# Batch 2's q and k loaded plain, cast by GpSimd and transposed on TensorE in a fused attention and MLP kernel

## The chip, the cores and the metric

The kernel runs on one core of one Trainium2 chip. The metric is the time of an execution on the device in microseconds (us); lower is better. The core's engines are TensorE (PE, with its weight loads counted apart as PEld), VectorE (DVE), ScalarE (ACT), GpSimd (POOL) and SyncE (SP, which here only issues DMAs). Each engine takes its instructions in the order in which the program wrote them, and waits where an operand isn't there yet.

## The reference

There are 8 batches of 8 heads, a sequence of 576 and a head dimension of 64, all inputs in float32. Per head:

```python
scores = q @ k.T / sqrt(64)
cum    = cumsum(log(clip(f, 1e-4, 1)))
scores = where(causal, -1e9, scores + cum[:, None] - cum[None, :])
attn   = softmax(scores)
out    = attn @ v
```

The heads of a token are put side by side, which gives x with 4608 rows of 512. Then `h = x @ w_in` (512 to 2048), `g = h * sigmoid(h)` and `g @ w_out` (2048 to 512), written in float32.

## The kernel before

**Units of work.** Attention goes by pairs of heads: pair p is batch p // 4, heads 2 (p % 4) and the next, 32 pairs in all. The MLP goes by groups of 512 tokens, 9 groups. A group has 16 parts of the first product (`m1_chunk`: four matmuls into hp at L397, tanh on ACT, one DVE instruction at L409 that writes gtile) and 16 parts of the second (`m2_part`: four matmuls into po at L422; every fourth part ends in a copy on ACT and an output store from SP, L435).

**Attention of a pair.** `scores` makes four score tiles (0 to 3): matmuls of kT by qT (L278), the exponential on ACT (L303), the causal mask on DVE (L317). `prep_v` on POOL multiplies v by the decay weights (L248). `attend_rows` is the product with v (L346), the division on DVE, and `turn_pair` transposes the result on PE (L368) and has ACT copy it into xT (L374). Group g of the MLP can start when xT of all its tokens is written: group 0 after batch 0, group 1 after batch 1, and so on.

**How q and k get into qT and kT.** Both need the head dimension on the partitions and bf16. There are two ways.

- Batches 0 and 1: `load_main` loads tokens 0 to 511 of q and k in float32 from SP's queue (L98) into `whole`, a buffer of the pool gpool under the tag gtile, which has two buffers and is shared with the MLP's gtile. `load_tail` does the same for the last 64 tokens (L107, two buffers). `cast_both(p)` has POOL cast a pair's share to bf16 (L190 for whole, L199 for the tails). `transposes(p, which)` makes five PE transposes (L232) and two DVE copies (L237, L241) of one of q and k.
- Batches 2 to 7: `load_qk` loads blocks of 128 tokens from POOL's queue with a cast to bf16 in the DMA (L123, into mp, 16 buffers); `turn_qk` issues a DMA transpose of a block from SP (L132) into qT or kT. A batch has five blocks, the last of 64 tokens, so ten casting loads and ten DMA transposes.

**The order around the change.** From pair 4 on, the loop over p writes out for each pair: what `plan` holds for p (DMA transposes and loads of v, all on SP); score tiles 0 and 1; n1 parts of the MLP; for pairs of batches 0 and 1, `transposes(p + 1, 0)`; `attend_rows(p - 1)` for the lower rows; `prep_v(p + 1)`; `cast_both(p + 2)` while p + 2 is below 8; what `fetch` holds for p (the casting loads, on POOL); score tiles 2 and 3; `transposes(p + 1, 1)`; and the rest of the MLP parts and of attention of the pair before. From batch 2 on, `attend_rows(p - 1)` comes after score tile 3 in one piece. `pace` sets how many MLP parts a pair gets, from the parts that are ready. For batch 2 the loads stand in fetch at pairs 4 (blocks 0, 1) and 5 (blocks 2 to 4), the transposes in plan at 6 (blocks 0, 1) and 7; for batch 3 the loads at 5, 6, 7 and the transposes at 8, 9, 10. The loads of v for batch 2 stand in plan at 4 (blocks 0, 1), 5 (block 2) and 6 (blocks 3, 4).

PSUM has four buffers under the tag big (pool pbig) for hp, po, the attention products and the transposes, and two for the score tiles.

Of the kernel before, what the change touches and what calls it, by code (L numbers as in the profile page):

```python
# [19 lines left out]
def kernel(  # L20
# [12 lines left out]
    B, H, S, D = q.shape  # L33
# [9 lines left out]
    NPB = H // 2  # L43
# [28 lines left out]
    tpool = ctx.enter_context(tc.tile_pool(name="tpool", bufs=3))  # L72
    opool = ctx.enter_context(tc.tile_pool(name="opool", bufs=4))
    NEARLY = 2
    NTURN = 4
    LAG = 10.0
    MOST = 9.0
# [8 lines left out]
    def raw_tile():  # L86
        return stp.tile([P, DM], FP32, name="raw", tag="raw")
# [4 lines left out]
    def load_main(b, h0, h1):  # L92
        if b not in whole:
            whole[b] = gpool.tile(
                [P, 2, H, (NB - 1) * D], FP32, name="whole", tag="gtile"
            )
        for which, src in enumerate((q, k)):
            nc.sync.dma_start(  # L98
                out=whole[b][:, which, h0:h1, :],
                in_=src[b, h0:h1, 0:SM, :].rearrange("h (p c) d -> p h (c d)", c=NB - 1),  # L100
            )

    def load_tail(b):
        for which, src in enumerate((q, k)):
            t = raw_tile()
            tails[b, which] = t.rearrange("s (h d) -> s h d", h=H)
            nc.sync.dma_start(  # L107
                out=tails[b, which][:TAIL, :, :],
                in_=src[b, :, SM:S, :].rearrange("h s d -> s h d"),
            )  # L110
# [86 lines left out]
    def cast_tail(b, j, which):  # L197
        m = cast[b, j, which]
        nc.gpsimd.tensor_copy(  # L199
            out=m[:TAIL, NB - 1, :, :], in_=tails[b, which][:TAIL, 2 * j : 2 * j + 2, :]  # L200
        )
# [236 lines left out]
    m2_queue = [(g, tb, pt) for g in range(NG) for tb in range(4) for pt in range(4)]  # L438
    m1_ready = 0
# [16 lines left out]
    def can_m1():  # L456
        if not m1_queue:
            return False
        g = m1_queue[0][0]
        return g < m1_ready and (not m2_queue or m2_queue[0][0] > g - 2)  # L460

    def can_m2():
        return bool(m2_queue) and (not m1_queue or m1_queue[0][0] > m2_queue[0][0])
# [14 lines left out]
    def have():  # L478
        return sum(1 for x in m1_queue + m2_queue if x[0] < m1_ready)

    def pace(p):
        b, j = divmod(p, NPB)
        if b < NEARLY:
            return have() / (NPB - j)
# [32 lines left out]
    def add(to, at, fn, *args):  # L517
        to.setdefault(at, []).append(lambda: fn(*args))

    for b in range(NEARLY, B):  # L520
        for i, group in enumerate([(0, 1), (2,), (3, 4)]):
            at = NPB * b - 4 + min(i, 1) if b == NEARLY else NPB * b - 7 + i
            for c in group:
                for w in range(2):
                    add(fetch, at, load_qk, b, c, w)
                    if b <= NEARLY + 1:
                        add(plan, at + (2 if b == NEARLY else 3), turn_qk, b, c, w)
                    elif i == 0 and b - 2 >= NTURN:
                        add(plan, NPB * b - 4, defer, 9.0, partial(turn_qk, b, c, w))
                    else:  # L530
                        add(plan, NPB * b - 4 + min(i, 1), turn_qk, b, c, w)
                add(plan, NPB * b - 5 + i + (b == NEARLY), load_v, b, c, nc.sync)

# [11 lines left out]
    with tc.manual_schedule():  # L545
        nc.scalar.dma_start(out=f_sb[:, :], in_=f.rearrange("b h s -> (b h) s"))
        load_main(0, 0, 2)
        load_tail(0)
        load_main(0, 2, 4)
        for c in range(2):  # L550
            load_v(0, c, nc.sync)
        load_main(0, 4, H)
        for c in range(2, NB):
            load_v(0, c, nc.sync)

        def cast_both(p):
            b, j = divmod(p, NPB)
            for w in range(2):
                cast_main(b, j, w)
            for w in range(2):  # L560
                cast_tail(b, j, w)

        make_identity(nc, ident_bf)
        make_upper_triangular(nc, mask01, val=1.0, diag=True)
        make_identity(nc, ident_f)
        for kT in kTs:
            nc.vector.memset(kT[:, :, S:], 0.0)
        for u in us:
            nc.vector.memset(u[:, :, uoff[4] + TAIL :], 0.0)
        for va in vaugs:  # L570
            nc.vector.memset(va[:, NB - 1, :, :], 0.0)
        nc.vector.memset(wT[:, NB - 1, :], 0.0)
        nc.vector.tensor_scalar(
            out=maskadd[:, :], in0=mask01[:, :], scalar1=1.0, scalar2=1e30,
            op0=ALU.subtract, op1=ALU.mult,
        )
        decay_clip()
        LO, HI = ((0, 3),), ((3, NB),)
        for w in range(2):
            cast_main(0, 0, w)  # L580
        for w in range(2):
            cast_tail(0, 0, w)
        cast_both(1)
        cast_both(2)
        load_w(w_in_bf, moe_w_in, 0, DFF // 2)
        load_w(w_in_bf, moe_w_in, DFF // 2, DFF)
        for w in range(2):
            turn_first(w)
        scores(0, 0)
        turn_first_tails()  # L590
        scores(0, 1)
        decay_sum()
        scores(0, 3)
        transposes(1, 0)
        scores(0, 2)
        decay_turn()
        prep_v(0)
        transposes(1, 1)
        scores(1, 0)
        cast_both(3)  # L600
        load_tail(1)
        load_main(1, 0, 4)
        load_main(1, 4, H)
        for c in range(NB):
            load_v(1, c, nc.sync)
        for p in range(1, NPB):
            more = p + 1 < NPB
            prep_v(p)
            scores(p, 1)
            if more:  # L610
                transposes(p + 1, 0)
            scores(p, 3)
            if more:
                transposes(p + 1, 1)
            if p > 1:
                turn_pair(p - 2)
            attend_rows(p - 1, LO)
            scores(p, 2)
            if more:
                scores(p + 1, 0)  # L620
            attend_rows(p - 1, HI)
        turn_pair(NPB - 2)
        attend_rows(NPB - 1, LO)
        attend_rows(NPB - 1, HI)
        m1_chunk(0, 0, begin=True)
        turn_pair(NPB - 1)
        m1_ready = 1
        cast_both(NPB)
        cast_both(NPB + 1)
        prep_v(NPB)  # L630
        for c in range(0, NFC, NFC // 4):
            load_rows(w_out_bf, moe_w_out, c, c + NFC // 4)
        work(HOLD)
        transposes(NPB, 0)
        work(1)
        transposes(NPB, 1)
        work(2)
        due = 0.0
        for p in range(NPB, NP):
            b, j = divmod(p, NPB)  # L640
            early = b < NEARLY
            for fn in plan.get(p, []):
                fn()
            due += pace(p)
            n = int(due)
            due -= n
            n1, n2 = (n + 2) // 3, (n + 1) // 3
            n3 = n - n1 - n2
            scores(p, 0)
            scores(p, 1)  # L650
            spend(0.4)
            work(n1)
            ahead = p + 1 < NPB * NEARLY
            rows = NPB < p < NPB * NEARLY
            if ahead:
                transposes(p + 1, 0)
            if rows:
                attend_rows(p - 1, LO)
                spend(0.6)
            if p + 1 < NP:  # L660
                prep_v(p + 1)
            if p + 2 < NPB * NEARLY:
                cast_both(p + 2)
            for fn in fetch.get(p, []):
                fn()
            if early:
                work(n2 // 2)
            scores(p, 2)
            scores(p, 3)
            spend(0.3)  # L670
            if ahead:
                transposes(p + 1, 1)
            if rows:
                attend_rows(p - 1, HI)
            work(n2 - n2 // 2 if early else n2)
            if b >= NEARLY and j > 0:
                attend_rows(p - 1)
                spend(1.2)
            work(n3)
            if j > 0 and b < NTURN:  # L680
                turn_pair(p - 1)
            if j == NPB - 1:
                attend_rows(p)
                spend(1.2)
                if b < NTURN:
                    work(2)
                    turn_pair(p)
                    ready(p)
                else:
                    retire(p)  # L690
        while m1_queue or m2_queue or later:
            n = len(m1_queue) + len(m2_queue)
            work(1)
            if n == len(m1_queue) + len(m2_queue):
                spend(1.0)
# [28 lines left out]
```

## Time and profile before

| what | value |
|---|---|
| median of 3 runs | 363.94 us (363.58 to 365.53) |
| the profiled execution: time | 366.61 us |
| the profiled execution: span from the first to the last instruction | 364.8 us |
| granted TensorE clock, mean | 0.984 |
| busy: PE, PEld | 339.6 us (93%), 167.1 us (46%) |
| busy: DVE, ACT, POOL | 189.7 us (52%), 212.1 us (58%), 120.5 us (33%) |
| chain that ended last | PE 75%, DMA 10%, SP's queue 7% |

All times below are from the start of the span. The view of 40 slices gives the busy share of each engine in tenths for each fortieth of the span (9.12 us), and the clock that the throttle granted to TensorE. A line of the timeline has the start, the duration from the first to the last instruction of a merged group, the engine, the line of the kernel, the operation, what it writes and reads (partitions x elements and type), how often, and in brackets the idle time before it with what ended it. A line of the waits has the waiting instruction, what it waited for, the sum in us, how many times, and the longest. Matmuls overlap, so the pace of a group is read from start to start. Pairs can be found in PE's timeline by their first score tile (64x512): pair 4 at 41.78, 5 at 49.46, 6 at 59.06, 7 at 67.72, 8 at 82.70, 9 at 95.10, 10 at 103.50, 12 at 123.22.

### The profile page before, as it was taken

How to read it: one execution, taken by the hardware profiler on the slowest of the kernel's cores; microseconds unless marked ns; L12 is line 12 of the kernel's file. 1: busy time of each engine (PE TensorE's matmuls, PEld its weight loads, DVE VectorE, ACT ScalarE, POOL GpSimd, SP SyncE). 2: the span in 40 equal slices, each digit the busy share in tenths (PEclk: the TensorE clock that was granted, in tenths of full speed). 3: DMA queues.
4: the chain of work that ended last, by engine and by line, in shares of the span. 5: the costliest groups of instructions: out<-in, count | busy, mean ns of one | idle time of the engine just before them, and what ended most of it. 6: DMA issues, size and time to landing. Idle time of an engine off the chain costs nothing.

```text
span 364.8 us, 7023 instructions
## 1 busy us (share of the span) xinstructions
PE 339.6 (93%) x2677; PEld 167.1 (46%) x2677; DVE 189.7 (52%) x442; ACT 212.1 (58%) x345; POOL 120.5 (33%) x204
## 2 busy tenths in 40 slices
PE   2798979947999999999999999999999999999995
PEld 1355435522455545554454444444544454444442
DVE  4764894422763387236832784358436832843410
ACT  4566764624974687567746784667367723744421
POOL 5563499466035704561454362011301000000000
PEclk9999999985999999999999999999999999999999
DMA  8899899999969799879979998453050014000012
GB/s 220 200 207 313 186 187 178 132 159 208 192 63 159 110 178 120 102 53 193 158 79 184 125 120 184 106 105 102 30 124 29 2 58 118 8 31 29 29 64 82
DMA packets 148082, 44.92 MB, mean 123 GB/s; under 512 B 136208, under 2 KB 142352, under 8 KB 148048
## 3 DMA queue, kind: packets, MB, share of 16 engines
q1 hardware_dynamic: 88544, 33.05, 42.3%
q0 software_dynamic: 59424, 11.28, 41.1%
q8 instruction: 21, 0.34, 0.4%
q10 hardware_dynamic: 80, 0.15, 0.1%
q14 instruction: 13, 0.11, 0.1%
HBM read 36.85 MB, written 9.44 MB: 127 GB/s over the span
## 4 chain that ended last, share of the span: by engine, by line
PE 75%; DMA 10%; SPq 7%; ACT 2%; POOL 2%; issue 1%; DVE 1%; ACTq 0%; DVEq 0%
PE hp L397 31%; PE po L422 31%; PE sc L278 6%; PE avr L346 6%; DMA w_out_bf<-in_moe_w_out_dram 3%; SPq L115 3%; DMA mp<-in_k_dram 3%; SPq L98 3%; SPq L132 2%; DMA qT<-mp 2%; ACT uT L303 1%; DMA vm<-in_v_dram 1%; DMA whole<-in_k_dram 1%; PE tpx L368 1%; POOL vaug L248 1%
## 5 line engine op out<-in xcount | busy, mean ns | idle before, releaser
L397 PE MATMUL hp<-xT,w_in_bf 128*128 128x512 bf16 x576 | 139.5, 385 | 1.1 <-ACT xT L374 0.7
L422 PE MATMUL po<-w_out_bf,gtile 128*128 128x512 bf16 x576 | 136.6, 379 | 0.9 <-DVE gtile L409 0.6
L409 DVE SCALAR_TENSOR_TENSOR gtile<-th,hp 128x512 bf16<-128x512 bf16 x144 | 96.3, 685 | 55.3 <-ACT th L408 53.1
L303 ACT ACTIVATE uT<-sc 128x1024 bf16<-128x1024 f32 (+1 forms) x128 | 101.2, 849 | 30.3 <-PE sc L278 21.6
L408 ACT ACTIVATE th<-hp 128x512 bf16<-128x512 f32 x144 | 85.0, 612 | 51.0 <-PE hp L397 48.2
L248 POOL TENSOR_TENSOR vaug<-vm,wT 128x512 bf16<-128x512 f32 x64 | 45.5, 733 | 140.7 <-PE avr L346 120.3
L397 PEld LDWEIGHTS <-w_in_bf 128*128 128x128 bf16 x576 | 53.5, 99 | 65.7 <-issue 8.6
L422 PEld LDWEIGHTS <-gtile 128*128 128x128 bf16 x576 | 53.6, 98 | 63.6 <-issue 3.2
L317 DVE TENSOR_TENSOR uT<-uT,mask 128x256 bf16<-128x256 bf16 (+1 forms) x112 | 35.8, 341 | 72.8 <-ACT uT L303 72.6
L431 ACT ACTIVATE osb<-po 128x512 f32<-128x512 f32 x36 | 21.7, 602 | 47.3 <-PE po L422 47.3
L278 PE MATMUL sc<-qT,kT 64*128 64x64 bf16 (+4 forms) x384 | 37.6, 288 | 12.2 <-DMA qT<-mp 6.5
L346 PEld LDWEIGHTS <-uT 128*128 128x128 bf16 x960 | 33.7, 98 | 7.1 <-issue 1.3
L346 PE MATMUL avr<-vaug,uT 128*128 128x65 bf16 x960 | 36.2, 195 | 0.7 <-POOL vaug L256 0.7
L278 PEld LDWEIGHTS <-kT 64*128 64x128 bf16 x384 | 15.1, 95 | 38.8 <-issue 24.0
L356 DVE TENSOR_TENSOR xt<-avr,rr 128x384 bf16<-128x384 f32 x64 | 31.4, 491 | 2.3
L123 POOL DMA_DIRECT2D mp<-in_q_dram x30 | 26.6, 887 | 0.0
L123 POOL DMA_DIRECT2D mp<-in_k_dram x30 | 25.9, 862 | 0.3 <-PE sc L278 0.3
L355 DVE RECIPROCAL rr<-avr 128x6 f32<-128x6 f32 x64 | 11.6, 182 | 19.0 <-PE avr L346 18.8
L374 ACT COPY xT<-tpx 128x512 bf16<-128x512 bf16 (+7 forms) x32 | 11.2, 404 | 17.2 <-PE tpx L368 17.2
L190 POOL CAST m<-whole 128x512 bf16<-128x512 f32 x16 | 9.8, 628 | 15.2 <-DMA whole<-in_q_dram 12.1
L368 PE MATMUL tpx<-ident_bf,xt 128*128 128x128 bf16 (+1 forms) x80 | 9.0, 216 | 1.3 <-DVE xt L356 1.1
L368 PEld LDWEIGHTS <-xt 128*128 128x128 bf16 (+1 forms) x80 | 6.2, 96 | 6.5 <-DVE xt L356 2.3
(47 smaller groups left out, 65.4 us busy)
## 6 DMA issues: line engine op xcount, KB each, us to landing
out_dram<-osb SPq DMA_DIRECT2D x36, 256.0 KB, 2.2
vm<-in_v_dram SPq DMA_DIRECT2D x32, 256.0 KB, 5.0
mp<-in_q_dram POOLq DMA_DIRECT2D x24, 128.0 KB, 5.5
mp<-in_k_dram POOLq DMA_DIRECT2D x24, 128.0 KB, 6.2
w_in_bf<-in_moe_w_in_dram POOLq DMA_DIRECT2D x2, 1024.0 KB, 11.2
w_out_bf<-in_moe_w_out_dram POOLq DMA_DIRECT2D x4, 512.0 KB, 9.7
whole<-in_q_dram SPq DMA_DIRECT2D x3, 512.0 KB, 10.9
whole<-in_k_dram SPq DMA_DIRECT2D x3, 512.0 KB, 9.6
```

The lines of the kernel that those rows point to most:

```text
L123: nc.gpsimd.dma_start(out=t[: bs[c], :].rearrange("p (h d) -> p h d", h=H), in_=(q, k)[which][b, :, c * P : c * P + bs[c], :].rearrange("h ...
L248: nc.gpsimd.tensor_tensor(out=va[:n, c0:c1, :, 0:D], in0=vm[:n, c0:c1, 2 * j : 2 * j + 2, :], in1=wT[:n, c0:c1, 2 * j + b * H : 2 * j + 2 ...
L278: nc.tensor.matmul(sc[:, i, col : col + n], lhsT=kT[r, kb * P : (kb + 1) * P], rhs=qT[r, q0 : q0 + n], start=True, stop=not pe_adds,)
L303: nc.scalar.activation(out=u[:, :, o : o + col], in_=sc[:, :, 0:col], func=ACT.Exp, scale=scale)
L317: nc.vector.tensor_tensor(out=d, in0=d, in1=mk, op=ALU.mult)
L346: nc.tensor.matmul(av[:, qb - lo, i, :], lhsT=u[:, i, o : o + P], rhs=va[:, kb, i, :], start=(kb == 0), stop=(kb == qb),)
L356: nc.vector.tensor_tensor(out=xt[:, lo:hi, 2 * j : 2 * j + 2, :], in0=av[:, :, :, 0:D], in1=r[:, 0:n, :, None].to_broadcast([P, n, 2, D]), ...
L397: nc.tensor.matmul(hp[:, :], lhsT=w_in_bf[:, cc, fc * P : (fc + 1) * P], rhs=xg[g][:, cc, :], start=(cc == 0), stop=(cc == NCC - 1),)
L408: nc.scalar.activation(out=th[:, :], in_=hp[:, :], func=ACT.Tanh, scale=0.5)
L409: nc.vector.scalar_tensor_tensor(out=gte[:, fc, :], in0=th[:, :], scalar=1.0, in1=hp[:, :], op0=ALU.add, op1=ALU.mult,)
L422: nc.tensor.matmul(po[:, :], lhsT=gte[:, fc, tb * P : (tb + 1) * P], rhs=w_out_bf[:, fc, :], start=(fc == 0), stop=(fc == NFC - 1),)
L431: nc.scalar.activation(out=osb[:, :], in_=po[:, :], func=ACT.Copy, scale=0.5)
```

## The change

Batch 2's q and k take the first way. A table RAW names, for batches 0 to 2, which of q and k (0, 1) do so. The loads of batch 2 into whole and the tails are issued on SP in pair 5, after the last cast of batch 1; the casts go to POOL in pairs 6 to 9 and the transposes to PE in pairs 7 to 10. Batch 2's ten casting loads and ten DMA transposes are not issued. Batch 3's casting loads are issued one pair later (pairs 6, 7, 8), and its DMA transposes at pairs 9 and 10. Since whole of batch 2 takes a gtile buffer, `can_m1` no longer lets group 1's first product start before group 0's second product is done.

```diff
+    RAW = {0: (0, 1), 1: (0, 1), 2: (0, 1)}
...
-        return g < m1_ready and (not m2_queue or m2_queue[0][0] > g - 2)
+        return g < m1_ready and (not m2_queue or m2_queue[0][0] > max(g - 2, min(g - 1, 0)))
...
     for b in range(NEARLY, B):
         for i, group in enumerate([(0, 1), (2,), (3, 4)]):
             at = NPB * b - 4 + min(i, 1) if b == NEARLY else NPB * b - 7 + i
+            late = 1 if b == NEARLY + 1 and len(RAW[NEARLY]) == 2 else 0
             for c in group:
                 for w in range(2):
-                    add(fetch, at, load_qk, b, c, w)
+                    if w in RAW.get(b, ()):
+                        continue
+                    add(fetch, at + late, load_qk, b, c, w)
                     if b <= NEARLY + 1:
-                        add(plan, at + (2 if b == NEARLY else 3), turn_qk, b, c, w)
+                        to = min(at + late + (2 if b == NEARLY else 3), NPB * b - 2)
+                        add(plan, to, turn_qk, b, c, w)
...
-            ahead = p + 1 < NPB * NEARLY
+            ahead = RAW.get((p + 1) // NPB, ())
             rows = NPB < p < NPB * NEARLY
-            if ahead:
+            if 0 in ahead:
                 transposes(p + 1, 0)
...
             if p + 1 < NP:
                 prep_v(p + 1)
-            if p + 2 < NPB * NEARLY:
+            if (p + 2) // NPB in RAW:
                 cast_both(p + 2)
+            if p == NPB * NEARLY - 3:
+                load_tail(NEARLY)
+                load_main(NEARLY, 0, 4)
+                load_main(NEARLY, 4, H)
             for fn in fetch.get(p, []):
                 fn()
...
-            if ahead:
+            if 1 in ahead:
                 transposes(p + 1, 1)
```

The other edits let `load_main`, `load_tail` and `cast_both` go over RAW[b] in place of both q and k, which is the same for these three batches.

More of the change, by code (lines that the diff above doesn't have):

```diff
@@ L96, in load_main @@
             )
-        for which, src in enumerate((q, k)):
+        for which in RAW[b]:
+            src = (q, k)[which]
             nc.sync.dma_start(
@@ L103, in load_tail @@
     def load_tail(b):
-        for which, src in enumerate((q, k)):
+        for which in RAW[b]:
+            src = (q, k)[which]
             t = raw_tile()
@@ L557, in cast_both @@
             b, j = divmod(p, NPB)
-            for w in range(2):
+            for w in RAW[b]:
                 cast_main(b, j, w)
-            for w in range(2):
+            for w in RAW[b]:
                 cast_tail(b, j, w)
```

## The prediction

> **What bounds the kernel now.** I read the 40-slice view first, then the table of waits, then the timeline of PE (TensorE) around the worst slice, then windows that put a number on it.
>
> ```profile
> PE   2798979947999999999999999999999999999995
> PEclk9999999985999999999999999999999999999999
> ```
>
> A slice is 9.12 us. From slice 10 (91 us) to the end PE is at 9 nearly everywhere: the span is PE's work laid end to end, so instructions added to PE cost their full time and idle time taken from it is gained in full. Before that, the hole is in slices 8 and 9 (73 to 91 us), where PE has 4 and 7 and the granted clock falls to 8 and 5.
>
> ```profile
> PE sc L278 <- DMA qT<-mp: 6.5, 2, 5.1
> ```
>
> The table of waits gives PE one large stall: the score matmuls (L278) wait twice, 6.5 us in all, for the DMA that turns q and k of a later batch into qT and kT.
>
> ```profile
> 74.84 0.52 PE L368 MATMUL tpx<-ident_bf,xt 128*128 128x128 bf16 x5
> 75.29 1.08 PE L346 MATMUL avr<-vaug,uT 128*128 128x65 bf16 x30
> ...
> 77.25 0.36 PE L368 MATMUL tpx<-ident_bf,xt 128*128 128x128 bf16 x2 [0.21 <-DVE xt L356]
> 82.70 0.61 PE L278 MATMUL sc<-qT,kT 64*128 64x512 bf16 x2 [5.09 <-DMA qT<-mp]
> 84.70 0.61 PE L278 MATMUL sc<-qT,kT 64*128 64x64 bf16 x4 [1.39 <-DMA qT<-mp]
> 85.25 5.15 PE L397 MATMUL hp<-xT,w_in_bf 128*128 128x512 bf16 x12
> ```
>
> It is the step from pair 7 to pair 8, the first of batch 2. No MLP work is left to fill it: 64 po matmuls, all 16 parts of group 0, stand before 75 us, and group 1 needs xT of batch 1, turned at 77.25. The 12 hp matmuls after it take 5.15 us, 0.43 each, against 0.225 elsewhere. The next rows price the whole:
>
> ```profile
> 41.78:49.46 7.68, 6.42 (x43) 2.85 (x43) 7.28 (x14) 6.29 (x10) 7.68 (x15) 1.00 0.94 159
> 77.61:85.25 7.64, 1.16 (x8) 0.27 (x7) 0.29 (x1) 1.73 (x3) 7.64 (x14) 0.65 2.39 129
> 85.25:90.33 5.08, 5.08 (x15) 1.65 (x14) 1.67 (x3) 2.22 (x3) 2.60 (x3) 0.52 1.72 245
> 95.10:98.34 3.24, 3.24 (x20) 1.31 (x20) 2.01 (x5) 3.13 (x5) 0.00 (x0) 1.00 0.65 142
> 95.10:103.50 8.40, 8.40 (x76) 4.29 (x76) 6.98 (x16) 6.74 (x12) 1.87 (x4) 1.00 0.73 145
> ```
>
> The columns are the stretch, its length, busy us (instructions) of PE, PEld, DVE, ACT, POOL, then the clock, DMA share, GB/s. Pair 8's first two score tiles and 12 hp matmuls take 7.64 + 5.08 = 12.72 us; the same 20 instructions of pair 9 take 3.24 (95.10 to 98.34). The hole costs 12.72 - 3.24 = **9.48 us**: 6.48 waiting, 3.0 slow work at clocks 0.65 and 0.52.
>
> **What the change removes.** Ten casting loads leave POOL (pairs 4 and 5; 3.65 + 5.11 us of its queue) and ten DMA transposes leave SP (pairs 6 and 7; 15.9 us from 60.10 to 82.1). Pair 8's scores then wait for DVE's copies of PE transposes placed in pair 7. If those come in time, 9.48 us go.
>
> **What it adds on PE.** Eight groups of five transposes, one for q and one for k in each of pairs 7 to 10. Batch 1 shows them:
>
> ```profile
> 61.36 0.52 PE L232 MATMUL tpqk<-ident_bf,m 128*128 128x128 bf16 x5
> 61.81 0.54 PE L346 MATMUL avr<-vaug,uT 128*128 128x65 bf16 x12
> ...
> 63.49 0.53 PE L232 MATMUL tpqk<-ident_bf,m 128*128 128x128 bf16 x5
> 63.95 0.72 PE L346 MATMUL avr<-vaug,uT 128*128 128x65 bf16 x18
> ```
>
> From the start of a group to the next instruction is 0.45 to 0.46 us; 8 x 0.455 = **3.64 us**, all on the path. The Trainium skill speaks against this step: "TensorE: Matmul & The Clock Gate", Part 4, puts a transpose at about 275 ns in a kernel, so that an estimate from that page is 40 x 0.275 = 11.0 us and the sum below would be -9.48 + 11.0 + 1.3 = +2.8 us. These rows have 0.09 us each when five follow one another, so the rows decide.
>
> **What it adds elsewhere.** DVE gets eight pairs of copies (0.68 + 0.175 us by L237 and L241), 1.71 us a pair of heads. In pair 9, DVE would have 6.98 + 1.71 = 8.69 us and PE 8.40 + 0.91 = 9.31: DVE at 93%. Pair 4 is such a stretch already: it has two groups of transposes among five hp chunks, DVE at 7.28 of 7.68, and PE waits 1.26 us at its end for DVE's kT copy. Pairs 7 and 10 are mostly po work (DVE 3.58 of 9.89 and 4.12 of 8.31 us), and batch 1's pairs 5 and 6, mostly po too, lose nothing to such copies. So the new waits lie between 0 and four times 1.26 = 5.0 us; I take **1.3**, one of the two hp-rich pairs (8 and 9) at pair 4's price. They include a buffer of the four in pbig held by a copy, and xT's copies on ACT (0.70 us at 77.65) ahead of pair 8's exponentials.
>
> POOL gets eight casts of whole (0.61 each) and eight of tails (0.29), 7.2 us, for 8.76 us of loads that leave it; SP issues six plain loads. They come at pair 5, behind batch 1's last cast, which holds their buffers:
>
> ```profile
> 47.34 1.38 POOL L190 CAST m<-whole 128x512 bf16<-128x512 f32 x2
> 48.68 0.52 POOL L199 CAST m<-raw 64x128 bf16<-64x128 f32 x2
> 49.15 0.95 POOL L123 DMA_DIRECT2D mp<-in_q_dram  x1
> ...
> 52.71 1.46 POOL L248 TENSOR_TENSOR vaug<-vm,wT 128x512 bf16<-128x512 f32 x2
> 54.20 1.18 POOL L190 CAST m<-whole 128x512 bf16<-128x512 f32 x2
> 55.30 0.54 POOL L199 CAST m<-raw 64x128 bf16<-64x128 f32 x2
> ```
>
> Without pair 4's loads, prep_v(6) starts at 49.15 instead of 52.71 and the last cast ends at 55.84 - 3.56 = 52.3. Batch 1's loads of the same sizes take 0.60, 0.60, 0.66, 0.58, 5.12 and 2.40 us to issue, so the tails and heads 0 to 3 are issued by 54.8. Such 512 KB loads land in 9.6 to 10.9 us (median), 12.9 at most: 64 to 68 us. The first reader is POOL's cast for pair 8, in pair 6, 1.9 us; the first PE transposes on it come in pair 7 behind eight po matmuls, at 70.0. Data are needed by 68.1: **0 us**, with a margin of 0 to 4. DMA is the unsure part: its row has 9 here, with w_out's loads landing until 57.8, but 14 casting loads that ran from 49.15 to 64.5 are gone from that stretch. What waits behind the cast on POOL: batch 3's first four loads (3.6 us), prep_v(8), cast 9, two more loads: done by about 77, and pair 9's transposes come at about 81.
>
> On SP, the wait for that cast holds up one output store (59.56 before) and v's last two blocks (issued from 66.59 before, behind four turns; now from about 63). The store has four buffers; v is no later. Heads 4 to 7 issue by 62.3 and, 10.9 us on, land at 73, for a cast of pair 8 and transposes in pair 9, at about 89.
>
> **Nothing** for the rest. Batch 3's last casting loads are issued at about 84, land at most 13.0 us later (the longest mp), and two turns (1.3 each, 9.2 to land) end at 109; scores(12, 0), at 123.22 before, comes at about 118.7. Whole takes a gtile buffer until pair 9's cast: group 1 then shares group 0's, read for the last time at 74.8, and group 2 starts after pair 11. The edit in can_m1 alters no order, since group 0 is done before group 1 is ready. The wait of 0.36 for w_out may go: 0 to 0.36, left at 0.
>
> **The sum.** -9.48 + 3.64 + 1.3 = -4.5 us. The profiled execution took 366.61 us (span 364.8, 1.8 around it) and would take 362.1. It is 2.7 above the median of the runs, 363.94; the difference is carried over: **359.4 us**.
>
> **Rivals.**
>
> Rival 1, DVE and ACT become the bound in batch 2. Each of four pairs waits 1.26: -9.48 + 3.64 + 5.04 = -0.8, 363.1 us. For it: DVE at 93% in pair 9, and in pair 4 two masks took 1.59 us beside POOL's work, against a mean of 0.33. Against it: DVE at half or less in pairs 7 and 10.
>
> Rival 2, slower: the load comes late. PE stands at pair 7's first transposes (70.0) until whole[2] is landed and cast. A delay of L costs L, and 3.0 more if the clock falls as after the 5.09 wait; waits of 1.26 cost no clock here. With 4.94 us of added work and waits, the change loses from L = 4.5 without that fall, from 1.5 with it. The Trainium skill's clock-gate page, Part 1, has the clock halved after about 3.4 us idle, which would put the turn at L = 3.4. At L = 5: +3.5, 367.4 us. For it: DMA's 9s, and casting loads that took 13.0 us there. Against it: the slowest landing of this load still just meets 68.1.
>
> Rival 3, all is hidden: DVE keeps up and the w_out wait goes. -9.48 + 3.64 - 0.36 = -6.2, 357.7 us. For it: pairs 5 and 6, which take such transposes with no wait for a copy.
>
> **How the numbers follow.** Forecast 0.58, rival 1 0.16, rival 2 0.14, rival 3 0.12. A difference of 0.5% (1.8 us) is about what a measurement here can tell: faster is the forecast and rival 3, 0.70; within it rival 1, 0.16; slower rival 2, 0.14. The range leaves out rival 2 alone: rival 3 to rival 1, 357.7 to 363.1, and 0.4 on each side, the distance of the lowest run from the median: 357.3 to 363.5.
>
> **What would show it.** PE's wait for the DMA qT gone from the table of waits at batch 2; the clock at 9 in slices 8 and 9; L232 with 110 matmuls instead of 70; scores of pair 8 within 0.5 us of the last tpx. The new waits, if any, name DVE's kT copy (L237) or ACT's th before hp matmuls at 78 to 96 us. A wait of PE at L232 for POOL's cast near 70 us shows rival 2, and the prediction wrong; so does a wait for DMA at scores(12, 0).

## The result and the profile after

| | before | after |
|---|---|---|
| median of 20 runs | 365.09 us | 362.72 us |
| lowest, highest | 363.58, 367.53 | 361.26, 367.60 |
| profiled execution: time, span, clock | 366.61, 364.8, 0.984 | 366.18, 364.4, 0.995 |

The ratio is 0.9939, interval [0.9916, 0.9962]: 2.2 us faster, where 4.5 was forecast. The ratio leaves out two slow executions of the changed kernel (367.01 and 367.60 us); the medians, which have them, differ by 2.4. The hole is gone, yet the two profiled executions differ by 0.4 us only. The rows of PE and of its clock in the 40-slice view of the changed kernel:

```profile
PE   2798969799999999999999999999999999999995
PEclk9999999899999999999999999999999999999999
```

Slices 8 and 9 are full, but slice 7 (64 to 73 us) has 7, and the clock falls there instead. PE's timeline of the changed kernel at the step from pair 7 to pair 8:

```profile
82.90 0.36 PE L371 MATMUL tpx<-ident_bf,xt 128*128 128x128 bf16 x2 [0.21 <-DVE xt L359]
83.07 0.63 PE L281 MATMUL sc<-qT,kT 64*128 64x512 bf16 x6
83.63 2.76 PE L400 MATMUL hp<-xT,w_in_bf 128*128 128x512 bf16 x11
```

Pair 8 follows the last tpx at once, at full pace, and pair 9 starts at 92.11 in place of 95.10. But pair 8 itself starts at 83.07, no earlier than the 82.70 at which the first of the two waits ended before: time was lost ahead of it. The same view around pair 7's start:

```profile
65.88 2.54 PE L425 MATMUL po<-w_out_bf,gtile 128*128 128x512 bf16 x11
70.05 0.34 PE L371 MATMUL tpx<-ident_bf,xt 128*128 128x128 bf16 x3 [1.64 <-DVE kT L244]
70.60 0.41 PE L371 MATMUL tpx<-ident_bf,xt 128*128 128x128 bf16 x2 [0.21 <-DVE xt L359]
70.78 1.08 PE L281 MATMUL sc<-qT,kT 64*128 64x512 bf16 x6
71.80 3.02 PE L425 MATMUL po<-w_out_bf,gtile 128*128 128x512 bf16 x8
```

PE waits 1.64 us for a DVE copy, and then eight po matmuls take 3.02 us where the kernel before needed 1.90 at the same place (68.28): the clock has fallen. Windows put it at 0.50 from 70.68 to 74.09, 3.41 us, and at 1.00 on both sides. What held DVE is in its own timeline of the changed kernel, and in GpSimd's:

```profile
65.77 3.52 DVE L320 TENSOR_TENSOR uT<-uT,mask 128x512 bf16<-128x512 bf16 x2 [1.03 <-ACT uT L306]
69.22 0.67 DVE L240 COPY kT<-tpqk 128x512 bf16<-128x512 bf16 x1
```

```profile
66.33 1.44 POOL L251 TENSOR_TENSOR vaug<-vm,wT 128x512 bf16<-128x512 f32 x2
67.68 0.25 POOL L259 CAST vaug<-wT 128x10 bf16<-128x10 f32 x1
67.81 1.17 POOL L193 CAST m<-whole 128x512 bf16<-128x512 f32 x2
68.92 0.53 POOL L202 CAST m<-raw 64x128 bf16<-64x128 f32 x2
```

Two causal masks, 0.55 us together elsewhere, last until 69.29; one of them alone takes 3.18 us. They end when GpSimd's multiplication for pair 8 and its casts for pair 9, which follow each other without a pause, are nearly over. The copy of kT behind them, and the PSUM buffer that it frees, come late by as much. In the kernel before, two masks met DMA issues of GpSimd (55.77 to 56.70) and took 0.55 us:

```profile
55.74 0.55 DVE L317 TENSOR_TENSOR uT<-uT,mask 128x512 bf16<-128x512 bf16 x2 [0.51 <-ACT uT L303]
```

**Theory 1**: masks wait for GpSimd's computing instructions, not for its DMA issues. The change replaces issues in pairs 4 and 5 by casts in pairs 6 to 9, so that computing instructions stand closer together and the masks of pairs 4 to 8 wait (14.2 us against 9.0). **Theory 2**, the rival: the waits ahead of pair 8 are chance, and the transposes and copies cost more than forecast.

The Trainium skill, "SBUF — State Buffer", section "SBUF: two separate sides", states that a VectorE instruction with two inputs in SBUF and a GpSimd instruction that reads SBUF contend for a shared pair of ports: the one that starts first has it for the whole instruction, and the other is blocked. The masks have two inputs in SBUF, and the 3.52 us above agree with a block. The page's rule is one instruction; here a mask waited through several. That the ports are the reason, no run here shows by itself.

### The profile page after: what moved, and what is told of

The parts are those of the page before. It is cut to its first block, busy times and chain, and to the rows that moved or that the text cites. A ratio compares the mean times of both kernels' runs of the same rounds, so it can differ in the third digit from the quotient of the medians.

```text
span 364.4 us, 7064 instructions
## 1 busy us (share of the span) xinstructions
PE 339.8 (93%) x2675; PEld 170.1 (47%) x2717; DVE 199.6 (55%) x458; ACT 212.1 (58%) x345; POOL 118.9 (33%) x210
## 4 chain that ended last, share of the span: by engine, by line
PE 80%; DVE 6%; ACT 4%; issue 3%; DMA 3%; SPq 2%; POOL 1%; POOLq 0%; ACTq 0%
PE po L425 33%; PE hp L400 30%; PE avr L349 7%; PE sc L281 6%; DVE uT L320 3%; PE tpx L371 2%; DVE gtile L412 2%; ACT uT L306 2%; ACT th L411 1%; DMA whole<-in_k_dram 1%; DMA xT<-xt 1%; SPq L100 1%; PE tpqk L235 1%; DVE xt L359 1%; DVE kT L240 0%
## 5 line engine op out<-in xcount | busy, mean ns | idle before, releaser
L400 PE MATMUL hp<-xT,w_in_bf 128*128 128x512 bf16 x556 | 135.6, 380 | 2.4 <-ACT xT L377 0.7
L425 PE MATMUL po<-w_out_bf,gtile 128*128 128x512 bf16 x554 | 134.6, 382 | 1.6 <-DVE gtile L412 0.4
L320 DVE TENSOR_TENSOR uT<-uT,mask 128x256 bf16<-128x256 bf16 (+1 forms) x112 | 40.3, 381 | 65.3 <-ACT uT L306 65.1
L126 POOL DMA_DIRECT2D mp<-in_q_dram x25 | 22.2, 889 | 0.0
L126 POOL DMA_DIRECT2D mp<-in_k_dram x25 | 21.5, 861 | 0.0
L193 POOL CAST m<-whole 128x512 bf16<-128x512 f32 x24 | 14.3, 608 | 17.9 <-DMA whole<-in_q_dram 13.2
L235 PE MATMUL tpqk<-ident_bf,m 128*128 128x128 bf16 (+1 forms) x110 | 12.7, 233 | 0.9 <-DVE gtile L412 0.8
```

The lines of the kernel that those rows point to most:

```text
L126: nc.gpsimd.dma_start(out=t[: bs[c], :].rearrange("p (h d) -> p h d", h=H), in_=(q, k)[which][b, :, c * P : c * P + bs[c], :].rearrange("h ...
L320: nc.vector.tensor_tensor(out=d, in0=d, in1=mk, op=ALU.mult)
L400: nc.tensor.matmul(hp[:, :], lhsT=w_in_bf[:, cc, fc * P : (fc + 1) * P], rhs=xg[g][:, cc, :], start=(cc == 0), stop=(cc == NCC - 1),)
L425: nc.tensor.matmul(po[:, :], lhsT=gte[:, fc, tb * P : (tb + 1) * P], rhs=w_out_bf[:, fc, :], start=(fc == 0), stop=(fc == NFC - 1),)
```

## The experiments

Times are compared with the kernel before on the same chip. A pair's length is from its first score tile to the next pair's.

**The changed kernel again** (no edit), on two chips.

> The changed kernel as it is, for a second profiled execution and its spans beside the granted clock. Theory 1 (DVE's causal masks wait while GpSimd's multiplications and casts follow each other without a pause, and PE waits for the copies behind the masks): ratio about 0.994; the masks of pairs 4 to 8 take well over 1.14 us a pair again (14.2 us in the first trace against 9.0 before), and PE waits for DVE's kT copy at pair 5 and in pair 6 or 7; an execution with less mask time has a shorter span. Theory 2 (the first trace's waits in pairs 4 to 7 are chance, the transposes simply cost more than 3.64 us): pairs 4 to 7 as long as before plus 0.9 us, and pairs 8 to 10 longer than 9.0, 9.5 and 9.0.

> The changed kernel again, on the same chip as the next three. Theory 1: its executions fall into two groups, at about 362.3 us with a clock of 0.997 to 1.0 and at about 366 with 0.991 to 0.995, as 20 and 12 of its 32 executions so far; ratio 0.992 to 0.996. Theory 2, that the upper group is chance of the chip: this chip may have no upper group.

Ratios 0.9961 [0.9928, 0.9995] and 0.9946 [0.9914, 0.9977]. With the first 20, there are 44 executions in two groups: 30 with a clock of 0.997 or more, median 362.0 us (the lower group, none above 363.84), and 14 with less, 364.1 to 367.6, median 365.9 (the upper group). The first profiled execution is of the upper group, the second (363.21 us, clock 1.0) of the lower. DVE's and GpSimd's timelines of the second, where the first has the lines above:

```profile
65.70 0.55 DVE L320 TENSOR_TENSOR uT<-uT,mask 128x512 bf16<-128x512 bf16 x2 [1.03 <-ACT uT L306]
```

```profile
66.60 1.45 POOL L251 TENSOR_TENSOR vaug<-vm,wT 128x512 bf16<-128x512 f32 x2
```

GpSimd starts 0.35 us after the masks have ended, where it started 0.56 us after the first had begun. Pair 6 takes 8.37 us against 10.58, pair 7 10.72 against 12.29. Between these two traces nearly 4 us go with a third of a microsecond in GpSimd's start against the masks. A third profile, of the run on the other chip (361.90 us, clock 1.0, lower group), shows that it isn't a matter of being early or late: there GpSimd starts at 64.79, closer behind the first mask, and the masks take 1.51 us, without a wait of PE in pair 6:

```profile
64.46 1.51 DVE L320 TENSOR_TENSOR uT<-uT,mask 128x512 bf16<-128x512 bf16 x2 [1.03 <-ACT uT L306]
```

Pairs 8, 9 and 10 take 9.04, 9.50 and 9.02 us in all three (within 0.01): theory 2 has no place there.

**Masks left out.** The same edit on both kernels:

```diff
-        if first:
+        if first or NPB <= p <= 2 * NPB:
             return
         if t == 2:
```

> The changed kernel with the causal mask left out for pairs 4 to 8 (work left out: 20 DVE instructions, about 5.7 us without any wait). Theory 1: PE's waits for DVE in pairs 4 to 7 go and with them the fall of the clock there; 3 to 5 us less than the changed kernel, ratio to before about 0.983. Theory 2: PE doesn't wait for the masks, at most 0.5 us less, ratio about 0.993.

> The kernel before with the causal mask left out for pairs 4 to 8 (work left out: 20 DVE instructions). Theory 1: PE's wait at the end of pair 4 (1.26 us) goes, little else, because GpSimd's computing instructions are parted by DMA issues here: 1 to 1.5 us less, ratio 0.996 to 0.998, against 2.3 us less for the same step on the changed kernel. Theory 2: as much less as on the changed kernel.

On the changed kernel 361.24 us, 0.9887 [0.9848, 0.9925], 2.3 us under the unedited one beside it; pair 4 takes 6.35 us in place of 7.94 to 9.23. That is less than the 3 to 5 expected. One of its six executions has a clock of 0.993 (362.99 us), so the clock can fall without these masks too. On the kernel before 1.0013 [0.9994, 1.0032]: no gain, though pair 4 takes 6.35 us there too. In the profiles the DMA turns end at a time of their own (the wait of pair 8 ends at 82.46 here, at 84.70 and 82.09 in two profiled executions of before), so what PE wins ahead of the hole it spends in it. By the ratios, then, the waits of pairs 4 to 7 cost nothing before, and count once the hole is gone. My expectation had this wrong.

**Issues put back between GpSimd's work.**

```diff
-                    add(fetch, at + late, load_qk, b, c, w)
+                    when = 4 if late and c == 0 else at + late
+                    add(fetch, when, load_qk, b, c, w)
...
+            if p == 2 * NPB - 1:
+                for fn in fetch.pop(p):
+                    fn()
             if (p + 2) // NPB in RAW:
                 cast_both(p + 2)
```

> The changed kernel with two casting loads of batch 3 (block 0) moved to pair 4, between a cast and a multiplication, and pair 7's two casting loads moved between multiplication and cast: DMA issues of 1.8 us again stand between GpSimd's computing instructions. Theory 1: the mask in front of pair 5's transposes waits less (1.9 us to about 0.6 to 1.2) and so does the one in pair 6 (3.5 to about 2); 1 to 3 us less than the changed kernel, ratio about 0.988. Theory 2: no difference, 0.994.

0.9927 [0.9898, 0.9955], median 362.74: 0.8 us under the unedited kernel beside it, at the edge of what can be told; 2 of its 12 executions have a clock below 0.997, against 5 of 12 beside it. Its profiled execution (366.38 us, clock 0.995) shows why it isn't cleaner: pair 6 is undisturbed (8.38 us), but GpSimd's casts and multiplication now run without a pause from 73.27 to 78.19, and two masks of pair 7 take 4.15 us, one of them 3.92. PE then waits 2.64 us for DVE, the clock is 0.50 for 3.42 us, and pairs 7 and 8 take 3.86 us longer than in the lower group. The collision moved by one pair.

**Casts on ScalarE**, meant to shorten GpSimd's runs: first five pairs, then only pairs 8 and 9 (condition `b == 2 and j < 2`).

```diff
-        nc.gpsimd.tensor_copy(
+        copy = nc.scalar.copy if b * NPB + j > 6 else nc.gpsimd.tensor_copy
+        copy(
             out=m[:, 0 : NB - 1, :, :].rearrange("p c h d -> p h c d"),
```

> The changed kernel with the 512-token casts of pairs 7 to 11 on ScalarE in place of GpSimd (ten casts, some 0.6 us each). Theory 1: GpSimd's runs shrink, the masks of pairs 5 to 8 fall towards 1.14 us a pair, PE waits less there, 1.5 to 3.5 us less than the changed kernel, ratio about 0.987, unless ScalarE (7.5 of 9.0 us busy in pair 8) becomes the bound in pairs 8 and 9, which would show as PE waiting for the exponentials. Theory 2: no gain, and 0 to 2 us more from ScalarE.

> The changed kernel with the 512-token casts of pairs 8 and 9 alone on ScalarE (issued in pairs 6 and 7, where ScalarE has room). Theory 1: the run of GpSimd that could hold up the masks of pair 6 shrinks from 3.1 to 2.0 us, no execution has the fall of the clock in pair 6 or 7, and pairs 8 and 9 take 9.04 and 9.50 us again: no run above 364, 0.3 to 0.7 us less than with all five pairs on ScalarE, ratio about 0.990. Theory 2: no better than the changed kernel, 0.995.

> The casts of pairs 8 and 9 on ScalarE, beside the changed kernel. Theory 1: no execution of the upper group (none above 364 with a clock of 0.995 or less), median 1.0 to 1.5 us under the changed kernel's. Theory 2: the same share in the upper group and the same median as the changed kernel.

With five pairs 0.9921 [0.9893, 0.9949]; with two 0.9935 [0.991, 0.9961] and 0.9921 [0.9892, 0.995], the latter 0.7 us under the unedited kernel beside it (361.20 and 361.87). None of 26 executions is in the upper group (highest 363.24 us), where the unedited kernel had 14 of 44. Two more, of the last run, took 369.64 and 575.54 us at clocks of 0.951 and 0.573, lower than in any execution of the unedited kernel; they are left out, and what made them is open. With five pairs ScalarE holds pairs 8 and 9 at 9.36 and 9.92 us; with two they are at 9.04 and 9.50. This is as theory 1 has it, in a smaller size on medians, since the median of the unedited kernel lies in its lower group. But the profiles give another reason than shorter runs. In all three, GpSimd's multiplication for pair 8 waits for v's load and starts at 67.5 to 68.0, 2.0 to 2.9 us after the masks, which take 0.55 or 0.56 us. GpSimd in the first run with two casts, whose masks stand at 65.52:

```profile
67.55 1.05 POOL L252 TENSOR_TENSOR vaug<-vm,wT 128x512 bf16<-128x512 f32 x1 [4.66 <-DMA vm<-in_v_dram]
```

So these runs show that the upper group goes when the two don't meet. That a shorter run of GpSimd would do it, they don't show.

**A forced collision.** Two loads moved behind pair 9's cast, and that cast done twice:

```diff
-                    add(fetch, at + late, load_qk, b, c, w)
+                    when = at + 2 if late and c == 1 else at + late
+                    add(fetch, when, load_qk, b, c, w)
...
+        for _ in range(2 if (b, j) == (2, 1) else 1):
```

> The changed kernel with two of the four casting loads that part GpSimd's cast of pair 8 from its multiplication for pair 8 moved behind the cast of pair 9, and that cast's 512-token part done twice (the same data again): GpSimd computes without a pause from about 64.8 to 69.3 us, across the masks of pair 6 (65.7 us) in every execution. Theory 1: all executions in the upper group, clock 0.995, about 366 us, ratio 1.000 to 1.004; masks of pair 6 above 3 us; PE waits 1.5 to 2 us for DVE in front of pair 7. Theory 2: the mixture of the changed kernel, ratio about 0.995.

0.998 [0.995, 1.001], but only 2 of 12 executions are above 365 us, as beside it: a miss. In its profile the multiplication for pair 8 didn't start at 64.8 but at 66.31. The profile puts the wait down to PE, which reads vaug's buffer for pair 5 until then; v's load landed at the same time (66.14), and the trace can't part the two. And the masks (66.11, 1.41 us for two) got in behind GpSimd's first instruction, though it went on computing until 70.8. When DVE gets its turn in such a run stays open.

**The transposes' price.** Pairs 9 to 11 use pair 8's q and k; their transposes and copies are left out.

> The changed kernel without the PE transposes and DVE copies of pairs 9 to 11 (their scores use pair 8's q and k; work left out: 30 transposes, 12 copies). Both theories take these six groups to cost 0.455 us each: 2.7 us less than the changed kernel in pairs 8 to 10, ratio about 0.987. If DVE's copies or the PSUM buffers cost more than PE's own time, 3.5 us or more less.

Pairs 8, 9 and 10 take 8.03, 8.40 and 8.31 us against 9.04, 9.50 and 9.02: 2.82 us for six groups, 0.47 each, with the small waits. (Its ratio, 0.9921 [0.9893, 0.9949], is from another chip than the unedited kernel's.) The 275 ns a transpose that the prediction cites from the Trainium skill ("TensorE: Matmul & The Clock Gate", Part 4) are not what this kernel pays, 0.094 us; the measurement decides.

The profile of this run (362.48 us, clock 0.994) is also a second trace with the long mask of pair 6, which lies ahead of the transposes left out:

```profile
64.65 3.51 DVE L322 TENSOR_TENSOR uT<-uT,mask 128x512 bf16<-128x512 bf16 x2 [1.03 <-ACT uT L308]
```

PE then waits 1.62 us for DVE's kT copy, the clock is 0.50 from 69.47 to 72.88, and pair 6 takes 10.61 us, as in the first profile (10.58). So the three profiled executions of changed kernels with a clock below 0.997 have a mask of 3.16 to 3.92 us each, and the six others that have these masks have none above 2.2. The two masks of pair 6 against GpSimd's start:

| run | GpSimd's start after the masks' | two masks take |
|---|---|---|
| forced collision | 0.20 us | 1.41 us |
| changed, third profile | 0.33 us | 1.51 us |
| changed, first profile | 0.56 us | 3.52 us |
| transposes left out | 0.74 us | 3.51 us |
| changed, second profile | 0.90 us | 0.55 us |

The rows fall in order, but they make no rule. Undisturbed, two masks end after 0.55 us, so in the fourth row they would have been done before GpSimd's recorded start; why they were held up there stays open.

**The kernel before again** (no edit).

> The kernel before, unchanged, for a second profiled execution. Theory 1: the hole between pairs 7 and 8 is there again but, the first profiled execution (366.6 us, clock 0.984) having been one of the longer ones, it costs 7.5 to 9 us in place of 9.48; the masks of pairs 4 to 8 take about 9 us; xT of batch 4 and the scores of pair 20 wait 0 to 1 us here too, if such late waits are chance. Theory 2: the hole costs 9.5 us again, and the smaller gain lies wholly in the changed kernel.

PE's timeline and windows of this execution (363.42 us, clock 0.991):

```profile
78.59 0.39 PE L278 MATMUL sc<-qT,kT 64*128 64x512 bf16 x2 [2.25 <-DMA qT<-mp]
82.09 0.61 PE L278 MATMUL sc<-qT,kT 64*128 64x64 bf16 x4 [3.11 <-DMA qT<-mp]
```

```profile
76.35:82.64 6.29, 0.94 (x7) 0.25 (x7) 1.24 (x1) 1.73 (x3) 6.29 (x11) 0.71 1.64 151
82.64:86.86 4.22, 4.00 (x14) 1.48 (x14) 1.11 (x3) 2.22 (x3) 3.77 (x6) 0.63 1.36 281
```

The same 20 instructions take 6.29 + 4.22 = 10.51 us here: the hole costs 10.51 - 3.24 = 7.27, not 9.48: 5.36 waiting and 1.91 slow work, where the first had 6.48 and 3.0. Windows show the clock at 0.50 for 6.83 us here (78.93 to 85.76) and for 10.24 us in the first profile (79.87 to 90.11), against 3.41 in the first profile of the changed kernel: two and three times 3.41. A mean clock of 1 - 0.5 x 3.41 n / 363 is 0.995, 0.991 and 0.986 for n of 1, 2 and 3, values that recur in the lists of runs; the first profile's 0.984 has 1.6 us of low clock at its end too, after PE's last work. So, as an estimate, the mean clock counts such stretches: the upper group of the changed kernel (0.995, 0.991) has one or two, its lower group none. Of 96 executions of the kernel before, 63 have a clock of 0.99 or more (median 364.4) and 33 less (365.7); three stretches or more, by a clock of 0.986 or less, have 24 (366.1).

**The second part of the change alone, and an accident.** I meant to put only the later loads of batch 3, with the turns of batch 3 that follow them, on the kernel before. The line that bounds the turns by pair `NPB * b - 2` has no effect on batch 2 in the change, which has none; on the kernel before it moved batch 2's last six turns from pair 7 to pair 6 as well. The next two runs part the two moves.

```diff
+            late = 1 if b == NEARLY + 1 else 0
...
-                    add(fetch, at, load_qk, b, c, w)
+                    add(fetch, at + late, load_qk, b, c, w)
...
-                        add(plan, at + (2 if b == NEARLY else 3), turn_qk, b, c, w)
+                        to = min(at + late + (2 if b == NEARLY else 3), NPB * b - 2)
+                        add(plan, to, turn_qk, b, c, w)
```

> The kernel before with the second part of the change alone: batch 3's casting loads one pair later. If the hole before pair 8 comes from batch 2's loads and turns sharing the DMA engines and GpSimd's queue with batch 3's loads, the hole shrinks by 1 to 4 us without a transpose on PE, ratio 0.990 to 0.997. If it is set by the ten loads and ten turns of batch 2 themselves, nothing changes: 1.000. Theories 1 and 2 of the changed kernel say nothing on this run.

> The run g1_late carried a second edit that its expectation didn't name: the bound of pair b*4 - 2 in the line for the turns also moved batch 2's last six DMA transposes from pair 7 to pair 6, ahead of one output store and two loads of v in SP's queue. This kernel is the one before with that move alone (loads of batch 3 as before). If SP's queue order made the hole: the six turns are issued at 66 to 76 us in place of 72 to 82, pair 8 starts within 0.5 to 1 us of the last tpx with no fall of the clock, 357.5 to 359 us, ratio 0.983 to 0.987. If batch 3's loads made it: 1.000.

> The kernel before with batch 3's casting loads one pair later and its own turns at pairs 9 and 10, batch 2's turns where they were: the second part of the change alone, as g1_late was meant to be. If SP's queue order made the hole: little, 0 to 1.5 us less, ratio 0.996 to 1.000. If batch 3's loads made it by filling GpSimd's queue and the DMA engines: 0.983 to 0.987.

> Both moves together, again, on the same chip as the two alone: ratio 0.981 to 0.988, about 358 us, 3 to 4 us under the changed kernel, with no transposes on PE and a clock of 0.998 to 1.0 in all executions.

Both moves: 0.9834 [0.9791, 0.9877] and 0.9806 [0.9781, 0.9831], 357.89 and 358.16 us. The turns of batch 2 alone: 0.9897 [0.9857, 0.9937], 360.75, a smaller gain than the 0.983 to 0.987 expected. Batch 3's loads and turns alone: 0.9966 [0.9945, 0.9986], 363.95. SP's queue before:

```profile
64.28 2.26 SPq L132 DMA_TRANSPOSE kT<-mp  x1
66.59 4.15 SPq L115 DMA_DIRECT2D vm<-in_v_dram  x2
70.83 0.94 SPq L435 DMA_DIRECT2D out_dram<-osb  x1
71.87 2.14 SPq L132 DMA_TRANSPOSE qT<-mp  x1
```

and in the second run with both moves, with PE's step to pair 8 there:

```profile
63.73 1.95 SPq L132 DMA_TRANSPOSE kT<-mp  x1
65.77 1.22 SPq L132 DMA_TRANSPOSE qT<-mp  x1
...
75.61 1.19 SPq L132 DMA_TRANSPOSE kT<-mp  x1
```

```profile
76.53 0.36 PE L368 MATMUL tpx<-ident_bf,xt 128*128 128x128 bf16 x2 [0.21 <-DVE xt L356]
76.74 0.39 PE L278 MATMUL sc<-qT,kT 64*128 64x512 bf16 x2
77.28 0.39 PE L278 MATMUL sc<-qT,kT 64*128 64x64 bf16 x4 [0.15 <-DMA qT<-mp]
```

Before, two loads of v and a store stood between the fourth turn and the fifth, and the last was issued until 82.1; with the turns in one piece it is 76.8, and pair 8's scores wait 0.15 us for a turn. So a good part of the hole was the order in SP's queue, and the rest lay with batch 3's loads and turns beside batch 2's (through which queue or engine, these runs don't tell): by medians the moves are worth 4.4 and 1.2 us alone, and 6.5 and 7.0 together. Against the changed kernel on the same chip, both moves take 357.89 us to 361.87, with no transpose added: the best version here.

## Why the prediction was wrong, point by point

Two steps failed: the hole's price, 2.2 us too high, which is the larger miss, and the swap of work on GpSimd, put at nothing in the sum, which held up DVE's masks. By luck the waits that were priced at 1.3 and hardly came made up for part of it.

- **The hole goes**: right. PE waits for no qT at pair 8, and the clock is 1.00 there.
- **"The hole costs 12.72 - 3.24 = 9.48 us"**: mis-sized, taken from one of the longer executions, with three stretches of low clock; a second, with two as in most executions, gives 7.27. Carried over to the median, the 9.48 was 2.2 too much. And 363.94, to which the difference was carried over, was the median of 3 runs; 20 gave 365.09.
- **"8 x 0.455 = 3.64 us, all on the path"**: right. Pairs 7 to 10 of the second profiled execution take 38.28 us, against 34.61 for before's without its hole (27.38 - 9.48 for pairs 7 and 8, 8.40, 8.31): 3.67, the new waits included.
- **"So the new waits lie between 0 and four times 1.26 ...; I take 1.3"** for pairs 7 to 10: the second profile has 0.2 us for a kT copy (95.12) and 0.2 for gtile in pair 8, and the lengths above leave 0.03. I expected DVE to be short of time where it had copies added; it wasn't.
- **"POOL gets eight casts of whole ... for 8.76 us of loads that leave it"**, with no term in the sum, is the step whose mechanism failed. Casts hold up masks, and issues didn't where they met (55.74). In 14 of 44 executions PE pays 3.9 us by the groups' medians; in the one of them that was traced it pays with a wait of 1.64 us in pair 6 and with the clock. I had the row for it, two masks at 1.59 us beside GpSimd's work, and used it only in rival 1, for the wrong pairs.
- **The load's landing, 0 us**: right with more margin than given. Pair 8's casts started at 60.16 and 61.66; pair 7's first transposes on them, at 74.65, waited for nothing.
- **"Nothing for the rest"**: right for batch 3. From pair 14 to the end the three profiled executions of the changed kernel take 227.3 to 228.2 us, two of before 226.5 and 226.8, with waits for xT and at pair 20 (up to 0.9 us). The kernel with both moves has 227.4 too, that with two casts on ScalarE 226.7 and 226.9. What sets this is open.

For the lower group the sum with these sizes is -7.27 + 3.67 + 0.5 to 1.6 (late) = -3.1 to -2.0; its median is 362.0 against 364.8 for the 96 executions of before, -2.8. The hole's price in it is that of one execution. The upper group takes another 1.2 off the mean gain (14/44 of 3.9). That a mask held up through GpSimd's run makes the upper group is shown by its absence where the two don't meet and by the traces (three with it, six without); how long a mask waits in a given run of GpSimd is not.

## What to carry to other kernels

Before work is moved to another engine to fill a stall, read the issuing queue of the stalled transfer: here two loads and a store that PE didn't wait for stood ahead of the last six turns, and two moves in the queues gained more than twice what the change did, at no cost on PE. Work that leaves an engine's queue and work that comes into it may last alike and still not be alike: ask what each shares with the engines beside it. A difference between two profiles of one kernel can mislead about its cause, so look at the same place in every trace there is. Size a stall from several executions, and remember that it hides waits ahead of it, which come back when it is gone.

## What the runs showed that was not expected

- Masks of 0.2 to 0.5 us took up to 3.9 us beside GpSimd's computing instructions, and PE felt it through DVE's copies.
- A wait of PE of 1.64 us, with 0.21 more and five transposes, was followed by a clock of 0.50 for 3.41 us; one of 1.81 us at 51.23 in the same execution was not. The prediction had the fall begin between 1.26 and 5.09.
- In five profiles the clock was low for one, two or three times 3.41 us, and executions of one program fall into groups by how often. In the changed kernel the groups lie 3.9 us apart.
